# Splitting of value rows and skip products moved off GpSimd in a gated S4 and PEER kernel

## The chip, the cores and the metric

The kernel runs on one NeuronCore of a Trainium2 chip. The core has five engines, each with an instruction stream of its own that it works through in order: TensorE (PE in the profile, its weight loads PEld), VectorE (DVE), ScalarE (ACT), GpSimd (POOL) and SyncE (SP), whose queue issues nearly all DMA transfers here. Streams meet only through semaphores. The metric is the device time of one execution in microseconds, lower being better. Before the change, three runs gave 1459.42, 1458.82 and 1459.39 us, a median of 1459.39 us.

## The reference

One sequence of 2048 tokens with 576 channels, all in fp32, goes through two blocks, and a gate per token mixes what they give:

```python
x = A_u                                             # (1, 2048, 576)
g = sigmoid((x * gate_w).sum(-1, keepdims=True))
a = irfft(rfft(K, 4096) * rfft(u, 4096))[:L] + u * Dskip   # S4: K from A, B, C, dt
# PEER: 32 heads, two sets of 64 subkeys, 64 * 64 = 4096 experts
q = einsum("nd,dhc->nhc", x, w_q)                   # two halves of 128
i1, t1 = top2(q1 @ k1.T);  i2, t2 = top2(q2 @ k2.T)
top_s, top_e = top2(of the four sums t1 + t2, and their experts)
b = einsum(softmax(top_s), gelu(x . u[top_e]), v[top_e])
out = g * a + (1 - g) * b
```

Two places matter here. The *skip product* is `u * Dskip`, one number per channel, added to the convolution. The *value rows* are `v`, 4096 rows of 576 numbers, one row per expert; the sum over the chosen experts weighs them.

## The kernel before, in words

**Products in halves.** TensorE works in fp16. An fp32 operand is scaled and split into a high half (the fp16 rounding) and a low half (the fp16 rounding of what is left); a product is then high x high, high x low and low x high. Tiles named `…hl` hold both halves. The high half is written by ScalarE (`vhl<-vhl,sci`), the low half by VectorE as scaled source minus high half in one instruction (`SCALAR_TENSOR_TENSOR`).

**Stages.** For about 900 us TensorE computes all scores (`s` groups) and the products of every token with every expert's `u` row (`a` groups; evicted as `go`, stored to `g_d` in DRAM), each group on two halves of 64 rows of the array that run beside each other. Between them run the convolution's Fourier stages; the product of the two spectra is made by `products`, whose result waits as `z_d` in DRAM. After `products`, `freq` opens the pool `ab` (L1426) and starts the last stage while the last `a` groups still run.

**The last stage** goes through 16 token tiles of 128 tokens in the order 0, 15, 1, 14 and so on, two tiles making a pair. For each tile, `prep` loads `gl` (two tiles of 1 MB, `gl_0` and `gl_1`), builds one-hot matrices on VectorE for each of four quarters of the heads (`A`, `Be`, and `Bg`, which is `Be` times the weights), has ScalarE apply Gelu to `gl`, and lets TensorE make `S = Bg x A` for the quarter in PSUM, by which VectorE multiplies `gl`. The first two quarters' one-hots are built ahead of the Gelu; those of quarter q+2 come behind the four multiplications of quarter q. Then `gl` is split into `wh_0` (ScalarE) and `wh_1` (VectorE), and 192 matmuls `o<-vhl,wh` of the tile sum over the experts. For each pair, `y_part` loads two tiles `ya` with the rows of `u`, `yz` and `tf`, multiplies `ya` by `db` (the channels' `Dskip`), waits for the inverse transform's `y` matmuls, adds them to `ya` on VectorE (`ya<-y,iuk,ya`), and ScalarE multiplies by the gate. `finish` adds the experts' sum (`ya<-o,om,ya`) and stores.

**Value rows** come in eight chunks of 512. `v_work` loads chunk c raw into the memory in which chunk c+1 will later be split (the last one into a tile `vs`), so chunk c+1 can't be loaded before chunk c is split. A chunk is four pieces of 128 x 576. The piece's high half is ScalarE's. The low half goes one of two ways, chosen at L1604 for each piece: ScalarE scales the raw piece in place (`vhl<-vhl,sci` with an fp32 result, or `vs<-vs,sci`) and GpSimd subtracts the high half; or VectorE does both in one instruction.

**What sets the order.** The program is written out by a planner that runs when it is built: work is a set of generators resumed by a model clock. Each engine has a model of when it will be free (`S.free`, `V.free`, `G.free`, from the cost functions), `ready(...)` waits until a tile is ready by that model, and a choice such as that of L1604 is made by these numbers. So a choice that falls differently also changes in which order later instructions are written. All engine calls go through the wrapper at L136, all matmuls through L216, and DMAs through L207; groups are told apart by their tiles. Waits between engines follow the data, whatever the order.

Of the kernel before, what the change touches and what calls it, by code (L numbers as in the profile page):

```python
# [140 lines left out]
def body(ctx: ExitStack, tc: tile.TileContext, xT, au, par, logdt, dskip, gatew, wq, kT, uT, vv,  # L141
# [5 lines left out]
    clock = [0.0]  # L147
# [15 lines left out]
    def size(x):  # L163
        n = 1
        for d in x.shape[1:]:
            n *= d
        return n
# [30 lines left out]
    S = Engine(nc.scalar, rdy, clock, key, act_cost)  # L198
    V = Engine(nc.vector, rdy, clock, key, dve_cost)
    G = Engine(nc.gpsimd, rdy, clock, key, lambda op, o, a, k: 0.15 + 0.0021 * size(o))  # L200

    def dma(o, i, q=None):
        t = max(clock[0], rdy.get(key(i), 0.0), queue[0])
        queue[0] = t + 0.45
        wire[0] = max(wire[0], t) + (2 if o.dtype in (F16, BF16) else 4) * o.shape[0] * size(o) / 3.4e5
        rdy[key(o)] = max(rdy.get(key(o), 0.0), wire[0] + 2.2)
        (q or DQ).dma_start(o, i)  # L207

    def mm(o, l, r, start, stop, cost=None):
        m = l.shape[0] > 64, 128 if size(l) > 64 else size(l)  # L210
        if m != tiling[0]:
            tiling[0] = m
            clock[0] += 0.13 if m == (True, 128) else 0.1
        clock[0] += (size(r) * (4 if r.dtype == F32 else 1) / 2400 + 0.003) if cost is None else cost
        rdy[key(o)] = clock[0] + 0.4
        return T.matmul(o, l, r, start=start, stop=stop)  # L216
# [73 lines left out]
    def ready(*xs, late=0.0):  # L290
        while True:
            t = max(rdy.get(key(x), 0.0) for x in xs) + late - clock[0]
            if t <= 0:
                return
            yield t
# [32 lines left out]
    def need(tag, n=1):  # L328
        while tag in banksets:
            lst = sorted(vacant)  # L330
            if held[tag] + n <= caps[tag] and len(lst) >= n and lst[n - 1][0] <= clock[0]:
                return
            yield max(0.2, min(0.3, lst[n - 1][0] - clock[0])) if len(lst) >= n else 0.3
        while True:
            lst = sorted(slots[tag])
            if len(lst) >= n and lst[n - 1] <= clock[0]:
                return
            yield max(0.2, lst[n - 1] - clock[0]) if len(lst) >= n else 0.3
# [6 lines left out]
    def free(tag, *outs, of=None):  # L345
        if of is not None:
            held[tag] -= 1
            vacant.append((max([clock[0]] + [rdy.get(key(x), 0.0) for x in outs]), number[of.tensor.name]))
            return
        if owed[tag]:  # L350
            owed[tag] -= 1
            return
        slots[tag].append(max([clock[0]] + [rdy.get(key(x), 0.0) for x in outs]))

    def done(gen):
        for _ in gen:
            return False
        return True
# [7 lines left out]
    def bank(tag, name):  # L366
        held[tag] += 1
        b = min(vacant)
        vacant.remove(b)
        t = ps.tile([128, 512], F32, tag=f"ps{b[1]}", name=name, bufs=1)  # L370
        number[t.tensor.name] = b[1]
        banks.add(t.tensor.name)
        return t
# [7 lines left out]
    def row(x, name, pool):  # L381
        t = pool.tile([128, D], F32, name=name)
        dma(t, bass.AP(tensor=x.tensor, offset=x.offset, ap=[[0, 128], [1, D]]))
        return t
# [7 lines left out]
    def au_load(a, t):  # L392
        for d, o in au_rows(au, t, a):
            dma(o, d)

    def pair_rows(x, n):

        return bass.AP(tensor=x.tensor, offset=x.offset + n * R1 * D, ap=[[D, R1], [32 * R1 * D, 4], [1, D]])
# [66 lines left out]
    def slot(shape, dt, name):  # L465
        take("slot", name)
        return bp.tile([128] + shape, dt, tag="s", name=name, bufs=9)
# [642 lines left out]
    ab = iota_a = iota_b = None  # L1110
# [288 lines left out]
    def freq():  # L1399
# [17 lines left out]
        KS.__exit__(None, None, None)  # L1417
        v_pool(0, 3)
        spawn(v_work())
        fp = FP.__enter__()  # L1420
        quota(sc=4, wb=5)
# [157 lines left out]
    def v_work():  # L1579
        raw = {}  # L1580

        def load(c):
            raw[c] = vt[c + 1].rearrange("p k z d -> p k (z d)").bitcast(F32) if c < 7 else slot([4, D], F32, "vs")
            r = 512 * c
            dma(raw[c], vv[r:r + 512].rearrange("(k p) d -> p k d", p=128))

        for c in range(8):
            while not vnormed or c not in vt or (c < 7 and c + 1 not in vt):
                yield 1
            if c not in raw:  # L1590
                if c == 7:
                    yield from need("slot")
                load(c)
            if c + 2 in vt or (c == 6 and done(need("slot"))):
                load(c + 1)
            h = vt[c]
            yield from ready(raw[c])
            for k in range(0, 4, 2):
                for j in (k, k + 1):
                    S.activation(h[:, j, 0, :], raw[c][:, j, :], AF.Copy, scale=sv[0])  # L1600
                yield from ready(h)
                for j in (k, k + 1):
                    x = raw[c][:, j, :]
                    if G.free < clock[0] + 1 and S.free < V.free:  # L1604
                        S.activation(x, x, AF.Copy, scale=sv[0])
                        yield from ready(raw[c])
                        G.tensor_sub(h[:, j, 1, :], x, h[:, j, 0, :])
                    else:
                        V.scalar_tensor_tensor(h[:, j, 1, :], x, sv[0], h[:, j, 0, :], op0=OP.mult, op1=OP.subtract)
            vhl.append(h)  # L1610
            yield 1
        free("slot", h)
# [80 lines left out]
    def y_part():  # L1693

        def load(p):
            ya = []
            for t in ORDER[2 * p:2 * p + 2]:
                a = oy.tile([128, D], F32, tag="ya", name=f"ya{t}", bufs=4)
                au_load(a, t)
                ya.append(a)  # L1700
            z = oy.tile([128, 4, D], F32, tag="yz", name=f"yz{p}", bufs=1)
            for j in range(4):
                dma(z[:, j], pair_rows(z_d, 4 * p + j))
            tf = oy.tile([128, 4, 64], F32, tag="tf", name=f"tf{p}", bufs=1)
            dma(tf, tf_d[:, 4 * p:4 * p + 4, :])
            return ya, z, tf

        db = row(dskip, "db", oy)
        nxt = load(0)
        for p in range(NT // 2):  # L1710
            ya, z, tf = nxt
            yield from ready(*ya, z, tf, late=4.0)
            for a in ya:
                G.tensor_mul(a, a, db)
            while p and ORDER[2 * p - 2] not in finished:
                yield 0.5
            yield from need("wb", 4)
            pbs = []
            for n in range(2):
                for hh in range(2):  # L1720
                    pb = bank("wb", f"y{p}_{n}_{hh}")
                    for j in range(4):
                        w = 3 - j if n else j
                        mm(pb[32 * j:32 * j + 32, :288], tf[:, w, 32 * n:32 * n + 32], z[:, w, 288 * hh:288 * hh + 288],
                           True, True, 0.13)
                    pbs.append(pb)
            for n, a in enumerate(ya):
                yield from ready(a, *pbs[2 * n:2 * n + 2])
                for hh in range(2):
                    ah = a[:, 288 * hh:288 * hh + 288]  # L1730
                    V.scalar_tensor_tensor(ah, pbs[2 * n + hh][:, :288], iuk, ah, op0=OP.mult, op1=OP.add)
                    free("wb", a, of=pbs[2 * n + hh])
                yield from ready(a)
                t = ORDER[2 * p + n]
                S.activation(a, a, AF.Copy, scale=gA[:, t:t + 1])
                yt[t] = a
            del pbs, pb
            if p + 1 < NT // 2:
                while p and ORDER[2 * p - 1] not in finished:
                    yield 0.5  # L1740
                nxt = load(p + 1)
# [132 lines left out]
    def choose(lst, ok):  # L1874

        near = [g for g in lst[:8] if ok(g)]
        return next((g for g in near if tb_of(g) % 2 != parity[0]), near[0] if near else None)
# [49 lines left out]
    while groups or acts:  # L1927
# [5 lines left out]
        a = choose(acts, a_fit)  # L1933
# [26 lines left out]
    until(lambda: len(placed) == NT)  # L1960
    oy = ctx.enter_context(tc.tile_pool(name="oy", bufs=1))
    spawn(y_part())
    for t in ORDER:
        until(lambda: t in st)
# [71 lines left out]
```

## Time and profile before

| | |
|---|---|
| runs | 1458.82, 1459.39, 1459.42 us; median 1459.39 |
| the profiled execution's own time | 1462.77 us |
| its span in the trace | 1461.0 us |
| TensorE busy | 1427.4 us, 98% of the span |
| VectorE busy | 1196.3 us, 82% |
| ScalarE busy | 837.1 us, 57% |
| GpSimd busy | 520.7 us, 36% |
| mean granted TensorE clock | 0.995 of full speed |

The profiled execution took 1.8 us more than its span and 3.4 us more than the median of the runs. Durations in the trace belong to that one execution. Rows of the trace name the engine, the line, the operation, the tile written and the tiles read (`out<-in`), partitions x elements, and after a count what the engine had waited for just before.

### The profile page before, as it was taken

The numbers are of one execution on the slowest core, as the hardware profiler recorded it, in microseconds if no ns is written. First come the engines' busy times: TensorE is split into PE (matmuls) and PEld (weight loads), VectorE is DVE, ScalarE is ACT, GpSimd is POOL, SyncE is SP. The second block draws the span as 40 slices with busy tenths as digits, with TensorE's granted clock in tenths as the row PEclk, the third lists the DMA queues.
The fourth block names the chain that finished last, engine by engine and source line by source line (L and its number), as shares of the span: only waits on it lengthen the run. The fifth ranks groups of instructions, "written<-read, shape, count | busy, mean of one in ns | idle before, by whom it ended". The sixth has DMA issues, their size and how long they took to land. (4 is left out here: it accounts for less than half of the span.)

```text
span 1461.0 us, 44118 instructions
## 1 busy us (share of the span) xinstructions
PE 1427.4 (98%) x17652; PEld 902.7 (62%) x17654; DVE 1196.3 (82%) x4573; ACT 837.1 (57%) x1452; POOL 520.7 (36%) x513
## 2 busy tenths in 40 slices
PE   7999999999999999999989999999999999999999
PEld 3465566554565665455654444446787887888787
DVE  5888699889889988767789997588989988998860
ACT  6547887987888887754656665574333224223310
POOL 0442265553472663431657899312010010110000
PEclk9999999999999999999999999999999999999999
DMA  9333543333341331248776788577343432442400
GB/s 312 121 113 99 161 129 110 107 119 111 115 147 47 120 109 45 81 141 270 264 252 201 261 269 302 180 242 229 112 148 117 135 119 92 131 148 68 156 9 17
DMA packets 134380, 215.89 MB, mean 148 GB/s; under 512 B 10912, under 2 KB 79904, under 8 KB 127776
## 3 DMA queue, kind: packets, MB, share of 16 engines
q1 hardware_dynamic: 134080, 213.01, 45.1%
q8 instruction: 138, 2.26, 0.6%
q14 instruction: 66, 0.54, 0.1%
q10 hardware_dynamic: 96, 0.07, 0.0%
HBM read 141.74 MB, written 71.30 MB: 146 GB/s over the span
## 5 line engine op out<-in xcount | busy, mean ns | idle before, releaser
L216 PE MATMUL s<-whl,xb 64*128 64x512 f16 x3072 | 469.0, 377 | 0.5 <-ACT k1o L136 0.3
L216 PE MATMUL a<-xb,uhl 64*128 64x512 f16 (+1 forms) x3024 | 457.9, 378 | 0.3 <-DVE go L136 0.2
L216 PE MATMUL o<-vhl,wh 128*128 128x288 f16 x3072 | 388.5, 287 | 0.0
L216 PEld LDWEIGHTS <-wh 128*128 128x128 f16 x3072 | 296.9, 98 | 76.3 <-issue 2.8
L216 PEld LDWEIGHTS <-xb 64*128 64x128 f16 x3456 | 226.5, 94 | 167.5 <-issue 14.5
L216 PEld LDWEIGHTS <-uhl 64*128 64x128 f16 (+1 forms) x3024 | 195.7, 94 | 167.3 <-issue 9.7
L136 ACT ACTIVATE wh<-gl,s_wg 128x1024 f16<-128x1024 f32 x64 | 68.7, 1137 | 195.6 <-DVE gl L136 195.6
L136 POOL TENSOR_TENSOR CS<-CS,ex 128x512 f32<-128x512 f32 x72 | 90.7, 1293 | 167.1 <-DVE ex L136 167.1
L136 POOL TENSOR_TENSOR ya<-ya,db 128x576 f32<-128x576 f32 x16 | 29.7, 1864 | 336.6 <-DMA ya<-in_au_dram 282.8
L216 PE MATMUL s<-wrem,xb 64*128 64x512 f16 x384 | 122.2, 376 | 0.0
L216 PE MATMUL a<-xb,wrem 64*128 64x512 f16 (+1 forms) x380 | 120.8, 379 | 0.0
L136 ACT ACTIVATE go<-a,i_a 128x512 f32<-128x512 f32 x97 | 66.2, 683 | 78.6 <-PE a L216 54.2
L136 DVE FIND_INDEX8 i<-m,s 128x8 uint32<-128x64 f32 x520 | 104.8, 221 | 0.0
L136 DVE SCALAR_TENSOR_TENSOR wh<-gl,s_wg,wh 128x1024 f16<-128x1024 f32 x64 | 91.5, 1459 | 13.4 <-ACT wh L136 13.4
L136 DVE TENSOR_TENSOR gl<-S,gl 128x256 f32<-128x256 f32 x256 | 90.3, 415 | 13.3 <-PE S L216 7.2
L136 POOL TENSOR_TENSOR e<-aN,rt 128x512 f32<-128x512 f32 x72 | 84.0, 1187 | 46.9 <-PE kb L216 46.8
L136 DVE FIND_INDEX8 i<-m,sx 128x8 uint32<-128x64 f32 x504 | 99.3, 217 | 0.0
L136 DVE MAX8 m<-s 128x8 f32<-128x64 f32 x520 | 74.2, 214 | 26.5 <-PE s L216 22.5
L136 DVE TENSOR_TENSOR Bg<-Be,vals 128x1024 f16<-128x1024 f16 x128 | 87.2, 722 | 2.2
L136 ACT ACTIVATE gl<-gl 128x1024 f32<-128x1024 f32 x64 | 63.6, 1045 | 43.6 <-DMA gl<-g_d 43.6
L136 DVE TENSOR_TENSOR A<-iota_a,vals 128x2048 f16<-128x2048 f16 x64 | 78.4, 1224 | 0.0
L136 ACT ACTIVATE CS<-CS 128x1024 f32<-128x1024 f32 x72 | 74.6, 1050 | 6.3 <-DVE CS L136 6.1
(209 smaller groups left out, 2435.0 us busy)
## 6 DMA issues: line engine op xcount, KB each, us to landing
g_d<-go SPq DMA_DIRECT2D x128, 256.0 KB, 2.5
gl<-g_d SPq DMA_DIRECT2D x32, 1024.0 KB, 5.6
wq<-in_wq_dram SPq DMA_DIRECT2D x16, 1152.0 KB, 6.1
su_d<-us SPq DMA_DIRECT2D x32, 288.0 KB, 2.6
sk_d<-k1o SPq DMA_DIRECT2D x32, 288.0 KB, 2.8
ui<-su_d SPq DMA_DIRECT2D x16, 576.0 KB, 4.2
ki<-sk_d SPq DMA_DIRECT2D x16, 576.0 KB, 5.7
vn<-in_vv_dram SPq DMA_DIRECT2D x32, 288.0 KB, 4.3
```

Of the source, the lines that this page charges most:

```text
L136: return f(*a, **k)
L216: return T.matmul(o, l, r, start=start, stop=stop)
```

## The change

Two conditions are edited. In `v_work`, a piece may take the way over ScalarE and GpSimd only as long as `ab` hasn't been opened, which is to say before `products` has ended. Chunks 2 to 7 of the value rows are all split behind it. In `y_part`, the product of `ya` with `db` is issued on VectorE in place of GpSimd.

```diff
@@ v_work
                     x = raw[c][:, j, :]
-                    if G.free < clock[0] + 1 and S.free < V.free:
+                    if ab is None and G.free < clock[0] + 1 and S.free < V.free:
                         S.activation(x, x, AF.Copy, scale=sv[0])
                         yield from ready(raw[c])
                         G.tensor_sub(h[:, j, 1, :], x, h[:, j, 0, :])
                     else:
                         V.scalar_tensor_tensor(h[:, j, 1, :], x, sv[0], h[:, j, 0, :], op0=OP.mult, op1=OP.subtract)
@@ y_part
             for a in ya:
-                G.tensor_mul(a, a, db)
+                V.tensor_mul(a, a, db)
```

Over the whole program this takes from GpSimd 9 subtractions and 16 products, and from ScalarE 9 scalings in place (7 of `vhl`, 2 of `vs`); VectorE gets 9 low halves and 16 products. By the planner's numbers one eviction of an `a` group (`go`) moves from VectorE to ScalarE. TensorE and SyncE have the same instructions as before; SyncE's are in the same order too.

The first place is VectorE's stream from the end of the first token tile to the one-hots and first multiplications of the second; `vhl_16491` is chunk 6 of the value rows (raw in `vhl_16492`), `vhl_16492<-vs` chunk 7. Before:

```order
L136 SCALAR_TENSOR_TENSOR vhl_16491<-vhl_16492,sci,vhl_16491 128x576
L136 TENSOR_TENSOR A_0_17224<-iota_a,vals 128x2048
L136 TENSOR_TENSOR Be_0_17226<-iota_b,vals 128x1024
L136 TENSOR_TENSOR Bg_0_17228<-Be_0_17226,vals 128x1024 x2
L136 TENSOR_TENSOR A_1_17231<-iota_a,vals 128x2048
L136 TENSOR_TENSOR Be_1_17233<-iota_b,vals 128x1024
L136 TENSOR_TENSOR Bg_1_17235<-Be_1_17233,vals 128x1024 x2
L136 SCALAR_TENSOR_TENSOR vhl_16491<-vhl_16492,sci,vhl_16491 128x576
L136 SCALAR_TENSOR_TENSOR vhl_16492<-vs,sci,vhl_16492 128x576
L136 TENSOR_SCALAR go_2_3_17362<-a_2_3_17278,i_a 128x512
L136 SCALAR_TENSOR_TENSOR vhl_16492<-vs,sci,vhl_16492 128x576
L136 TENSOR_TENSOR gl_0_17220<-S_0_0_17383,gl_0_17220 128x32x8
```

After:

```order
L136 SCALAR_TENSOR_TENSOR vhl_16491<-vhl_16492,sci,vhl_16491 128x576 x2
L136 TENSOR_TENSOR A_0_17242<-iota_a,vals 128x2048
L136 TENSOR_TENSOR Be_0_17244<-iota_b,vals 128x1024
L136 TENSOR_TENSOR Bg_0_17246<-Be_0_17244,vals 128x1024 x2
L136 TENSOR_TENSOR A_1_17249<-iota_a,vals 128x2048
L136 TENSOR_TENSOR Be_1_17251<-iota_b,vals 128x1024
L136 TENSOR_TENSOR Bg_1_17253<-Be_1_17251,vals 128x1024 x2
L136 SCALAR_TENSOR_TENSOR vhl_16492<-vs,sci,vhl_16492 128x576 x4
L136 TENSOR_TENSOR gl_0_17238<-S_0_0_17381,gl_0_17238 128x32x8
```

All of chunk 6 now stands ahead of the one-hots, all four pieces of chunk 7 behind them, and the eviction `go_2_3` has left VectorE.

The second place is ScalarE's stream at the same point, up to the Gelu of the second tile (`gl<-gl`). Before:

```order
L136 ACTIVATE vhl_16492<-vhl_16492,sci 128x576
L136 ACTIVATE vhl_16492<-vs,sci 128x576 x2
L136 ACTIVATE go_2_2_17292<-a_2_2_17188,i_a 128x512
L136 ACTIVATE vs<-vs,sci 128x576
L136 ACTIVATE vhl_16492<-vs,sci 128x576 x2
L136 ACTIVATE go_1_1_17330<-a_1_1_17244,i_a 128x512
L136 ACTIVATE vs<-vs,sci 128x576
L136 ACTIVATE gl_0_17220<-gl_0_17220 128x1024 x2
L136 ACTIVATE gl_1_17221<-gl_1_17221 128x1024 x2
```

After:

```order
L136 ACTIVATE vhl_16492<-vs,sci 128x576 x4
L136 ACTIVATE go_2_2_17289<-a_2_2_17182,i_a 128x512
L136 ACTIVATE go_1_1_17322<-a_1_1_17219,i_a 128x512
L136 ACTIVATE go_2_3_17353<-a_2_3_17273,i_a 128x512
L136 ACTIVATE gl_0_17238<-gl_0_17238 128x1024 x2
L136 ACTIVATE gl_1_17239<-gl_1_17239 128x1024 x2
```

The scalings in place are gone from ahead of the Gelu, and `go_2_3` has come in.

The third place is the skip product in the steady part of the last stage, here of the fourth pair on VectorE. Before, the products of all pairs stand on GpSimd one behind the other (here those of the first two pairs, behind chunk 7), and the stream holds nothing else from there to its end:

```order
L136 TENSOR_TENSOR vhl_16492<-vs,vhl_16492 128x576 x2
L136 TENSOR_TENSOR ya_17554<-ya_17554,db 128x576
L136 TENSOR_TENSOR ya_17559<-ya_17559,db 128x576
L136 TENSOR_TENSOR ya_17947<-ya_17947,db 128x576
L136 TENSOR_TENSOR ya_17952<-ya_17952,db 128x576
```

After, on VectorE, between the one-hots of the last quarter and the multiplications by `S_3`:

```order
L136 TENSOR_TENSOR Bg_3_19534<-Be_3_19532,vals 128x1024 x2
L136 TENSOR_TENSOR gl_0_19315<-S_2_0_19567,gl_0_19315 128x32x8
L136 TENSOR_TENSOR gl_1_19316<-S_2_0_19567,gl_1_19316 128x32x8
L136 TENSOR_TENSOR gl_0_19315<-S_2_1_19584,gl_0_19315 128x32x8
L136 TENSOR_TENSOR gl_1_19316<-S_2_1_19584,gl_1_19316 128x32x8
L136 TENSOR_TENSOR ya_19357<-ya_19357,db 128x576
L136 TENSOR_TENSOR ya_19362<-ya_19362,db 128x576
L136 TENSOR_TENSOR gl_0_19315<-S_3_0_19637,gl_0_19315 128x32x8
```

So a pair's two products now stand in line with VectorE's other work, and nothing of the last stage is left on GpSimd. TensorE's stream differs in two stretches: seven row halves of the last `a` groups stand ahead of the second tile's first `S` in place of behind it, and in the first four tiles of the last stage the `o` matmuls are shared out differently between the `S` and `y` groups. From the fifth tile on it is the same.

## The prediction

> **What bounds the kernel now.** I read the page's busy shares first, then windows of the stage that the change touches, then the waits of TensorE in it.
>
> ```profile
> PE 1427.4 (98%) x17652; PEld 902.7 (62%) x17654; DVE 1196.3 (82%) x4573; ACT 837.1 (57%) x1452; POOL 520.7 (36%) x513
> ...
> core 0: us, PE busy (x) PEld busy (x) DVE busy (x) ACT busy (x) POOL busy (x), PEclk, DMA share, GB/s
> 1105.00:1162.00 57.00, 57.00 (x674) 46.20 (x673) 50.71 (x81) 17.88 (x18) 3.74 (x2) 1.00 0.37 119
> 940.00:970.00 30.00, 28.16 (x323) 13.70 (x319) 24.19 (x33) 19.89 (x27) 5.73 (x4) 1.00 0.84 281
> ```
>
> TensorE bounds it. In a pair's period of the last stage (the 1105 row) it is busy 57.00 of 57.00 us, while VectorE has 6.3 us to spare there. Where the value rows are split (the 940 row) TensorE loses 1.84 us in 30. The edited instructions run on other engines, so the change can pay only what TensorE waits for today and can cost only new waits. TensorE's timeline from 943 us to the end shows four waits of over 0.3 us, all for the one-hots `Bg` of VectorE:
>
> ```profile
> 963.74 0.20 PE L216 MATMUL S<-Bg,A 128*128 128x64 f16 x1 [0.36 <-DVE Bg L136]
> 965.41 1.10 PE L216 MATMUL S<-Bg,A 128*128 128x64 f16 x31 [1.48 <-DVE Bg L136]
> ...
> 1001.72 0.59 PE L216 MATMUL a<-xb,wrem 64*128 64x512 f16 x2
> 1003.68 0.20 PE L216 MATMUL S<-Bg,A 128*128 128x64 f16 x1 [1.37 <-DVE Bg L136]
> 1004.28 1.10 PE L216 MATMUL S<-Bg,A 128*128 128x64 f16 x31 [0.40 <-DVE Bg L136]
> 1005.22 5.51 PE L216 MATMUL o<-vhl,wh 128*128 128x288 f16 x30
> ...
> 1031.69 1.10 PE L216 MATMUL S<-Bg,A 128*128 128x64 f16 x31 [0.39 <-DVE Bg L136]
> 1085.06 1.09 PE L216 MATMUL S<-Bg,A 128*128 128x64 f16 x31 [0.41 <-DVE Bg L136]
> 1085.99 3.84 PE L216 MATMUL o<-vhl,wh 128*128 128x288 f16 x30
> ```
>
> The first gap is 0.36 + 1.48 = 1.84 us (the third quarter's `S` of tile one), the second 1.37 + 0.40 = 1.77 us (the same of tile two). Behind the second, 30 `o` matmuls took 5.51 us; the same 30 behind the small wait at 1085 took 3.84. The granted clock says why:
>
> ```profile
> 1005.50:1006.00 0.50, 0.50 (x5) 0.30 (x2) 0.50 (x2) 0.00 (x0) 0.00 (x0) 0.50 0.00 0
> 1008.50:1009.00 0.50, 0.50 (x5) 0.33 (x4) 0.46 (x5) 0.00 (x0) 0.00 (x0) 0.69 0.81 277
> ```
>
> TensorE ran at half clock from about 1005.5 to 1008.7 us, which cost 5.51 - 3.84 = 1.67 us. So all that can be won is 1.84 + 1.77 + 1.67 + 0.39 + 0.41 = 6.1 us, 0.4% of the time.
>
> **What the moved instructions cost, and what they stop costing.**
>
> ```profile
> L136 DVE SCALAR_TENSOR_TENSOR vhl<-vhl,sci,vhl x21: 803/812/1834, 913.0 to 993.4; 128x576 f16<-128x576 f32 x21
> L136 POOL TENSOR_TENSOR ya<-ya,db x16: 1397/1906/2487, 1010.5 to 1362.5; 128x576 f32<-128x576 f32 x16
> L136 DVE TENSOR_TENSOR tt<-tt 128x512 f32<-128x512 f32 x9 | 10.2, 1129 | 0.6
> ...
> 947.23 1.29 DVE L136 TENSOR_TENSOR Bg<-Be,vals 128x1024 f16<-128x1024 f16 x2
> 962.98 2.38 DVE L136 TENSOR_TENSOR Bg<-Be,vals 128x1024 f16<-128x1024 f16 x2
> 963.15 1.66 POOL L136 TENSOR_TENSOR vhl<-vhl,vhl 128x576 f16<-128x576 f32 x1 [8.23 <-ACT vhl L136]
> ...
> 1121.55 2.48 DVE L136 SCALAR_TENSOR_TENSOR wh<-gl,s_wg,wh 128x1024 f16<-128x1024 f32 x2 [0.94 <-ACT wh L136]
> 1133.64 3.63 DVE L136 SCALAR_TENSOR_TENSOR wh<-gl,s_wg,wh 128x1024 f16<-128x1024 f32 x2
> 1133.92 2.27 POOL L136 TENSOR_TENSOR ya<-ya,db 128x576 f32<-128x576 f32 x1 [0.76 <-DVE Bg L136]
> ```
>
> The first rows give minimum, median and maximum ns. A low half is 0.81 us on VectorE, so nine more are 9 x 0.81 = 7.3 us. But a GpSimd product that runs beside VectorE holds it up by about its own length: the pair of `Bg` at 962.98 took 2.38 us beside a GpSimd subtraction, 1.29 without one; the pair of `wh` at 1133.64 took 3.63 beside a skip product, 2.48 without one. That is 1.09 and 1.15 us for each. Taking nine subtractions off GpSimd so gives VectorE back up to 9 x 1.09 = 9.8 us, and one eviction has left VectorE too. Its load in the splitting stage is about what it was (between 7.3 us more, were there no hold-up, and 2.5 less); I take none.
>
> A skip product in fp32 on VectorE isn't in the trace. From below it is the low half of the same size, 0.81 us; from above the fp32 row of 512 columns, 1.13 x 576/512 = 1.27 us, which includes what hold-up those had. I take 0.8, since the low half too reads two operands of this very size: 16 x 0.8 = 13 us over the last stage (20 at the upper end), against 16 x 1.15 = 18 us of hold-up gone. For a pair that is 1.6 to 2.5 us more and 2.3 less, in a period with 6.3 us free. The cost on the path is nothing, covered by VectorE's spare time:
>
> ```profile
> DVE ya L136 <- PE o L216: 16.3, 10, 1.9
> DVE wh L136 <- ACT wh L136: 9.4, 10, 0.9
> DVE gl L136 <- PE S L216: 5.5, 6, 1.2
> ```
>
> These are VectorE's waits over the five periods from 1105 to 1390 us, 31.2 us or 6.2 a period, half of them for TensorE itself. Without this cover each us would come back as a TensorE wait.
>
> The skip products now make VectorE wait in order for the DMA that brings `ya`; queued behind them stand the multiplications by `S_3`, and TensorE waits for `wh` behind these.
>
> ```profile
> 1131.69 1.47 POOL L136 TENSOR_TENSOR ya<-ya,db 128x576 f32<-128x576 f32 x1 [52.16 <-DMA ya<-in_au_dram]
> 1145.96 2.76 DVE L136 TENSOR_TENSOR gl<-S,gl 128x256 f32<-128x256 f32 x8
> ```
>
> GpSimd had its second tile by 1133.92 at the latest; the place on VectorE is inside the run of eight that starts at 1145.96, about 13 us later. No wait there: 0.
>
> **First gap.** ScalarE's and VectorE's rows ahead of it:
>
> ```profile
> 952.79 2.09 ACT L136 ACTIVATE vhl<-vhl,sci 128x576 f32<-128x576 f32 x3
> 956.20 3.90 ACT L136 ACTIVATE gl<-gl 128x1024 f32<-128x1024 f32 x4
> ```
>
> The three scalings in place directly ahead of the Gelu go. The high halves that take their place in line wait for four low halves on VectorE, so I count 1.7 of the 2.09 us as won. Then the `Bg` pair that TensorE waited for loses its hold-up of 1.09 us: 1.7 + 1.09 = 2.8 us, against a gap of 1.84. Closed: 1.84 us, about 1 us in hand.
>
> **Second gap.** Its chain today:
>
> ```profile
> 993.40 0.81 DVE L136 SCALAR_TENSOR_TENSOR vhl<-vhl,sci,vhl 128x576 f16<-128x576 f32 x1
> 994.25 0.78 ACT L136 ACTIVATE vhl<-vs,sci 128x576 f16<-128x576 f32 x1 [4.10 <-DVE vhl L136]
> 996.17 3.88 ACT L136 ACTIVATE gl<-gl 128x1024 f32<-128x1024 f32 x4
> 1000.08 1.08 DVE L136 TENSOR_TENSOR gl<-S,gl 128x256 f32<-128x256 f32 x3 [1.46 <-ACT gl L136]
> 1002.93 1.29 DVE L136 TENSOR_TENSOR Bg<-Be,vals 128x1024 f16<-128x1024 f16 x2
> ...
> gl<-g_d SPq DMA_DIRECT2D x1, 1024.0 KB, 9.1
> ```
>
> Chunk 6's last low half stands behind both one-hots, so ScalarE sits 4.10 us and the Gelu starts at 996.17. It ends at 1000.05; the last `Bg` ends at 1004.22, 4.17 us later. In the new order chunk 6 is done before the one-hots and the scalings are out of line, so ScalarE is held by nothing of the split; what is late next is the second `gl` load (issued at 986.92, landed 996.0) and the eviction `go_2_3` that has come in. With TensorE 1.84 us ahead, the stores ahead of that load, and the load, move up by as much, to 994.2; the Gelu of the first tile can fill the time before. It then ends at 996.6 to 997.1 and the last `Bg` at 1000.8 to 1001.3. TensorE, 1.84 us earlier, comes for it at 1002.31 - 1.84 = 1000.5. A gap of 0.3 to 0.8 stays; I take 0.5 and a gain of 1.77 - 0.5 = 1.3 us.
>
> **Half clock.** A gap of half a us did not bring it: at 1031.69 and 1085.06, 0.4 us, 30 `o` took 3.84 behind the latter. I count its 1.67 us as won. The Trainium skill's TensorE: Matmul & The Clock Gate, Part 1 (The HAM clock gate), speaks against this: the clock falls after an idle window of some 3.4 us and the windows run free of the kernel. No gap here is that long, the 1.84 us of the first was followed by full clock (1.00 in the 940 row), and the 1.77 of the second by half. By that rule the drop hangs on more than the gap's length, and the sum would be without the 1.67 us.
>
> **Small gaps.** The 0.39 and 0.41 us come from VectorE being late by that much. The first pair's skip products leave GpSimd beside it; I take half, 0.4 us.
>
> Sum: 1.84 + 1.3 + 1.67 + 0.4 = 5.2 us. The profiled execution took 1462.77 us, 1.8 over its span and 3.4 over the median; it would become 1457.6, and the median 1459.39 - 5.2 = 1454.2 us. Differences under 0.2% (2.9 us) can hardly be told from none here.
>
> **The rivals.**
>
> *The drop isn't the gap's doing* (the page's rule, as a mechanism of this kernel: it falls on the same stretch or another one). Gains 1.84 + 1.3 + 0.4 = 3.5, so 1455.9. For it: the equal gap at 963 without a drop. Against it: the drop began right with the end of the second gap.
>
> *The second gap stays.* The `gl` load lands no earlier than today's 996.0, its Gelu ends near 998, the last `Bg` at 1002.2, and the gap is again 1.7 us against a TensorE that comes at 1000.5; the half clock then stays as well. Gain 1.84, so 1457.5. For it: the load took 9.1 us in a stretch of heavy DMA traffic (0.84 in the 940 row). Against it: ScalarE's 4.10 us wait is certainly gone.
>
> *VectorE becomes the bound* (slower). In the steady periods a pair costs it 1.6 to 2.5 us more, none is returned, and the skip products stand where TensorE's next `wh` hangs. Were its 6.2 us no real cover, as half of it is waiting for TensorE, seven periods would cost up to 7 x 2.5 = 17 us and at 1 us each 7: with 3.5 gained, 1463 to 1473, say 1465. It decides once `ya` lands over 13 us later or VectorE's slack ahead of `wh` is under 1.6 us. Against it: the returned hold-up, and TensorE's 57.00 of 57.00.
>
> **How the numbers follow.** The forecast 45%, the drop apart 20%, the second gap 23%, the slower case 10%, and 2% for a little more than the sum (all gaps gone, 1453.3). The first, second and last lie under 1456.5: faster 0.64 after a little spread over the bounds. The third gives same, 0.26, with what spreads from the others; slower 0.10. The range goes from 1452.8 (all 6.1 us, and half a us for the runs) to 1459.6 (no change), leaving out the slower case and little else.
>
> **What would show it.** Right: no waits on `Bg` near 962 and under 0.8 us near 1000, granted clock 1.00 from 1000 to 1010, `Bg` pairs at 1.29 throughout, GpSimd idle through the last stage, `ya<-ya,db` on VectorE near 0.8 us without a DMA wait, and 57.00 of 57.00 for TensorE in the steady periods. Wrong: a clock drop elsewhere, ScalarE waiting for `gl<-g_d` ahead of the second Gelu, or new waits of TensorE on `wh` or `y` after 1020. The `y` matmuls too come some 4 us earlier, at 1017, and their table `tf` with them, as far as SyncE's stores have moved up.

## The result and the profile after

The changed kernel takes 1452.66 us (median of six runs, 1451.91 to 1457.09), against 1459.41 us for the kernel before on the same chip: a ratio of 0.9957, 95% interval 0.9944 to 0.9971. That is 6.75 us less, where the prediction had 5.2; the time lies 0.14 us under the low end of its range. On a second chip both were run again: 1453.40 against 1460.59 us, ratio 0.9953 (0.9938 to 0.9968), 7.2 us less.

The page's busy shares of the profiled execution (span 1450.1 us, 1451.91 us in all), and the windows that the prediction showed of before, with one more:

```profile
PE 1422.8 (98%) x17654; PEld 902.6 (62%) x17654; DVE 1193.5 (82%) x4597; ACT 830.3 (57%) x1444; POOL 477.1 (33%) x488
```
```profile
core 0: us, PE busy (x) PEld busy (x) DVE busy (x) ACT busy (x) POOL busy (x), PEclk, DMA share, GB/s
1105.00:1162.00 57.00, 57.00 (x689) 46.30 (x686) 50.79 (x85) 17.88 (x18) 0.00 (x0) 1.00 0.36 119
940.00:970.00 30.00, 30.00 (x365) 15.16 (x363) 26.62 (x45) 17.71 (x24) 0.00 (x0) 1.00 0.86 281
1000.00:1010.00 10.00, 10.00 (x108) 8.20 (x106) 9.90 (x21) 4.27 (x4) 0.00 (x0) 1.00 0.79 211
```

TensorE is busy in all of 940 to 970 us and runs at full clock from 1000 to 1010, where before it was busy for 8.24 of the 10 us at a granted clock of 0.83. VectorE's load in a steady period is what it was, 50.79 us after 50.71 (150.39 after 150.98 over the three windows from 1105 to 1276 us), though a pair has two more instructions there: what it got and what GpSimd no longer takes from it cancel.

TensorE's timeline at the places of the four gaps:

```profile
958.77 1.14 PE L216 MATMUL S<-Bg,A 128*128 128x64 f16 x32
...
995.12 0.59 PE L216 MATMUL a<-xb,wrem 64*128 64x512 f16 x2
995.64 0.20 PE L216 MATMUL S<-Bg,A 128*128 128x64 f16 x1
996.11 1.10 PE L216 MATMUL S<-Bg,A 128*128 128x64 f16 x31 [0.27 <-DVE Bg L136]
...
1024.58 1.10 PE L216 MATMUL S<-Bg,A 128*128 128x64 f16 x31 [0.21 <-DVE Bg L136]
...
1076.37 1.13 PE L216 MATMUL S<-Bg,A 128*128 128x64 f16 x32
1077.34 3.84 PE L216 MATMUL o<-vhl,wh 128*128 128x288 f16 x30
```

The first gap is gone. Of the second 0.27 us are left, of the third 0.21, of the fourth nothing.

**The two profiles can't be subtracted as they stand.** Their spans differ by 10.9 us, more than the medians do. In the profile of before TensorE had also waited 1.72 us for `vo` at 913 us and run at half clock behind it, ahead of anything that the change moves; its first `S` starts at 955.12, that of after at 950.58. Executions of one kernel differ by a few us in that way before the last stage begins. So below, an execution is measured from the start of the first `S` to the end of the span, and cut at two places on TensorE's timeline: the first `o` and the first `y`; the last cut is the last `S`. From that to the end it was 57.7 us in every kernel. (The `before again` row is from an experiment below.)

| us | first S to first o | to first y | to last S | first S to end of span |
|---|---|---|---|---|
| before | 50.10 | 16.69 | 381.39 | 505.88 |
| before again | 50.46 | 16.28 | 381.89 | 506.33 |
| after | 46.47 | 15.02 | 380.37 | 499.52 |
| after again | 46.47 | 15.02 | 380.00 | 499.20 |

By this the change is worth 6.4 to 7.1 us, as the medians have it: 3.6 to 4.0 in the first part (the two gaps), 1.3 to 1.7 in the second (the half clock), 1.0 to 1.9 in the third. In `before again` the half clock begins at 999.99 us, ahead of the first `o` at 1000.83, so some 0.4 us of it stand in its first part.

### The profile page after: what moved, and what is told of

The parts are those of the page before. It is cut to its first block, busy times and chain, and to the rows that moved or that the text cites. A ratio compares the mean times of both kernels' runs of the same rounds, so it can differ in the third digit from the quotient of the medians.

```text
span 1450.1 us, 44027 instructions
## 1 busy us (share of the span) xinstructions
PE 1422.8 (98%) x17654; PEld 902.6 (62%) x17654; DVE 1193.5 (82%) x4597; ACT 830.3 (57%) x1444; POOL 477.1 (33%) x488
## 4 chain that ended last, share of the span: by engine, by line
PE 86%; DMA 5%; DVE 4%; issue 1%; SPq 1%; ACT 1%; POOL 1%; ACTq 0%; POOLq 0%; DVEq 0%
PE a L216 25%; PE o L216 24%; PE s L216 21%; PE S L216 4%; PE kb L216 2%; PE pr L216 2%; PE wb L216 2%; DMA wq<-in_wq_dram 1%; SPq L207 1%; PE kP L216 1%; PE y L216 1%; DVE i L136 1%; PE pv L216 1%; DVE m L136 1%; PE u L216 1%
## 5 line engine op out<-in xcount | busy, mean ns | idle before, releaser
L136 DVE SCALAR_TENSOR_TENSOR wh<-gl,s_wg,wh 128x1024 f16<-128x1024 f32 x64 | 79.7, 1278 | 10.4 <-ACT wh L136 10.4
L136 DVE TENSOR_TENSOR Bg<-Be,vals 128x1024 f16<-128x1024 f16 x128 | 82.7, 688 | 2.2
L216 PEld LDWEIGHTS <-A 128*128 128x128 f16 x2048 | 70.1, 97 | 6.4 <-issue 2.8
```

Of the source, the lines that this page charges most:

```text
L136: return f(*a, **k)
```

## Experiments

Each kernel was timed in five rounds beside the kernel before on the same chip (before: 1461.48 us for the first four, 1460.59 for the next four, 1461.82 for the last four), and profiled once.

**The split edit alone.** The diff against the kernel before:

```diff
-                    if G.free < clock[0] + 1 and S.free < V.free:
+                    if ab is None and G.free < clock[0] + 1 and S.free < V.free:
```

> Only the edit of v_work; the skip products stay on GpSimd. Theory (the gain is that of the two gaps on Bg and of the half-clock stretch behind the second, all in the stage where the value rows are split): 5 to 6 us less than before, the waits at 963 and 1002 us gone or under 0.5 us, full clock from 1000 to 1010; the small waits of 0.4 us at 1031 and 1085 stay. Rival (the gain comes from GpSimd being free beside VectorE through the last stage): under 2 us less than before.

1457.89 us, ratio 0.9982 (0.9968 to 0.9995): 3.6 us less. The parts of the last stage are 46.46, 15.03 and 384.36 us, 503.50 in all. The first two parts are those of the changed kernel: both gaps shut, no half clock. But of the 5.3 us that they give, 2.7 are lost in the third (384.36 against 381.39 and 381.89). TensorE's timeline of this kernel behind the first `y`:

```profile
1016.49 2.15 PE L216 MATMUL y<-yz,tf 128*32 128x288 f32 x32
1018.57 1.14 PE L216 MATMUL S<-Bg,A 128*128 128x64 f16 x32
1019.54 0.90 PE L216 MATMUL o<-vhl,wh 128*128 128x288 f16 x6
1021.62 1.12 PE L216 MATMUL S<-Bg,A 128*128 128x64 f16 x32 [1.17 <-DVE ya L136]
1022.58 4.57 PE L216 MATMUL o<-vhl,wh 128*128 128x288 f16 x36
1028.66 0.20 PE L216 MATMUL S<-Bg,A 128*128 128x64 f16 x1 [1.50 <-DVE Bg L136]
1029.26 1.10 PE L216 MATMUL S<-Bg,A 128*128 128x64 f16 x31 [0.40 <-DVE Bg L136]
```

TensorE, 5.3 us ahead of before at `y` (61.5 us behind the first `S` in place of 66.8), now waits there for VectorE: 1.17 us until `ya<-y` frees a bank and 1.90 for the third tile's `Bg`. Half of the gain is lost again one tile on. Theory right on the gaps, wrong in taking them for the edit's whole effect.

**The skip edit alone.**

```diff
-                G.tensor_mul(a, a, db)
+                V.tensor_mul(a, a, db)
```

> Only the edit of y_part; the value rows are split as before. Theory: 0.4 to 0.8 us less than before, which the runs can hardly tell from nothing: both gaps on Bg of 1.8 us and the half clock behind the second stay; VectorE's pairs of wh take 2.48 us throughout. Rival: 4 us less or more. Where VectorE has no room for the products: 3 us more or worse.

1458.72 us, ratio 0.9986 (0.9975 to 0.9996): 2.8 us less by the medians. In the profile 50.10, 15.02 and 379.99 us. The third part has lost all its waits, 1.4 to 1.9 us. Both gaps stay, and the second this time has no half clock behind it:

```profile
1000.84 0.20 PE L216 MATMUL S<-Bg,A 128*128 128x64 f16 x1 [1.36 <-DVE Bg L136]
1001.44 1.10 PE L216 MATMUL S<-Bg,A 128*128 128x64 f16 x31 [0.40 <-DVE Bg L136]
1002.38 3.84 PE L216 MATMUL o<-vhl,wh 128*128 128x288 f16 x30
```

So by the profile the skip edit is worth about 1.5 us by itself; the rest of its median lies within the scatter. That a gap of 1.76 us at this place passes without half clock was not expected.

**The kernel before, again** (unchanged).

> The kernel before, unchanged, for a second profile. In the first one TensorE also waited 1.72 us for vo at 913 us, ahead of anything that the change moves, and ran at half clock for some 7 us behind it; the changed kernel's profile has neither. Theory: that was this one execution (it took 3.4 us more than the median), so it is absent here, and the time is near 1459.4 with a mean clock of 0.998 or so. Rival: it is in every execution of the kernel before, and the changed kernel gained there too. The gaps at 963 and 1002 us are in both, by both.

1461.13 us, ratio 0.9998 (0.9987 to 1.0010). The wait for `vo` is 0.56 us here, without half clock behind it, so the first profile's was of its execution. The two gaps are as they were, and half clock stands behind the second again. But the mean clock over the runs is 0.995, not 0.998: this profile has half clock near 597, 686 and 744 us too, ahead of the change and in other executions elsewhere. All fourteen profiles have one such stretch or more between 590 and 760 us, at places that change, and they go with the scatter: over the 35 runs of before beside these four kernels, the runs with a lower mean clock are the longer ones (correlation -0.74).

**The gap put back.** In the changed kernel, for `t == ORDER[1]` and `q == 2` (the two runs at the end of this section have `range(1)`, and `ORDER[0]` with `range(5)`, in place of these):

```diff
         V.tensor_tensor(out=Be, in0=iota_b[:, None].to_broadcast([128, 8, 64, 2]), in1=ib(1, 64), op=OP.is_equal)
+        if t == ORDER[1] and q == 2:
+            for _ in range(3):
+                nc.vector.tensor_tensor(out=Be, in0=iota_b[:, None].to_broadcast([128, 8, 64, 2]), in1=ib(1, 64), op=OP.is_equal)
```

> The changed kernel, with VectorE building Be three times more, to the same result, ahead of the Bg that the third S of the second tile waits for: 3 x 0.6 = 1.8 us. TensorE's wait there grows from about 0.4 to 2.1 us, the length that it had before or a little more. Theory (a gap of 1.8 us at this place brings the half clock): about 1.8 us for the gap and 1.7 for the clock, 3.5 in all over the changed kernel, and a granted clock under 0.9 in the 3 us behind it. Rival (the drop before came from elsewhere): 1.8 us more and full clock.

1457.76 us, ratio 0.9983 (0.9971 to 0.9995): 4.4 us over the changed kernel's 1453.40 on that chip, or 3.5 when each is taken against its own series of the kernel before. TensorE's timeline, and windows behind the gap (the granted clock is the third number from the end):

```profile
998.78 0.24 PE L216 MATMUL S<-Bg,A 128*128 128x64 f16 x1 [1.98 <-DVE Bg L136]
999.38 1.81 PE L216 MATMUL S<-Bg,A 128*128 128x64 f16 x31 [0.36 <-DVE Bg L136]
```
```profile
1000.00:1002.50 2.50, 2.50 (x30) 1.97 (x28) 2.46 (x5) 0.00 (x0) 0.00 (x0) 0.50 0.61 122
1002.50:1005.00 2.50, 2.50 (x12) 1.59 (x11) 2.46 (x8) 0.00 (x0) 0.00 (x0) 0.50 0.73 223
```

A gap of 2.34 us brought half clock, and for 6.8 us, not 3.4. From first `S` to end of span the kernel takes 504.02 us, 4.5 to 4.8 over the changed one. That is the theory's case, if anything over its 3.5: a gap of this length here costs more than itself.

**The changed kernel, again** (unchanged).

> The changed kernel, unchanged, on the same chip as the next ones. Theory: as on the first chip, 6 to 7 us less than before (some 1454 to 1455 where before takes 1461), with no wait on Bg over 0.5 us in the profile and no half clock between 995 and 1010 us. Rival (part of the first result was the chip's or the executions' scatter): 4 to 5 us less.

1453.40 us, 7.2 us less than before; no gap over 0.3 us and no half clock behind the first `S`. The first result holds on a second chip.

**The order of the changed kernel, the skip products on GpSimd.**

```diff
+                V.eng = nc.gpsimd
                 V.tensor_mul(a, a, db)
+                V.eng = nc.vector
```

The planner still counts them as VectorE's, so every engine's order is that of the changed kernel; only the products themselves are on GpSimd.

> The order of the changed kernel on every engine, with the skip products issued on GpSimd at the same places. It tells the engine from the order. Theory (the order, in which 18 o matmuls stand between y and the next S, is what keeps TensorE fed here, the engine is worth about 1 us): 1 to 1.5 us slower than the changed kernel, by a wait on Bg of 1 to 1.5 us near 1025 us. Rival (the engine is what counts): as slow as the split edit alone, 3 us over the changed kernel, with a wait for ya behind y.

1454.00 us, ratio 0.9957 (0.9940 to 0.9975): 0.6 us over the changed kernel, not told from it, and less than the 1 to 1.5 expected. The parts are 46.47, 15.68 and 380.67 us; the wait for `Bg` near 1026 us is 0.40 us, not 1 to 1.5, and the second part holds a wait of 0.58 us at `y`.

**The order of the split edit alone, the skip products on VectorE.** The same exchange of the engine, on the kernel with only the split edit:

```diff
+                G.eng = nc.vector
                 G.tensor_mul(a, a, db)
+                G.eng = nc.gpsimd
```

> The order of the kernel with the split edit alone on every engine, with the skip products issued on VectorE at the places where they were issued on GpSimd: the other corner of the same square. Theory: S right behind the first y still waits for the bank that ya<-y sets free, now behind the two products, but VectorE comes there 2.3 us earlier without GpSimd's hold-up: waits of 0.3 us for ya and some 0.7 for Bg in place of 1.17 and 1.90, so about 2 us less than the split edit alone. Rival: no gain over the split edit alone.

1456.77 us, ratio 0.9970 (0.9957 to 0.9984): 1.1 us less than the split edit alone by the medians, 0.2 against each one's own series of the kernel before: not told from it, where 2 less was expected. The parts are 46.46, 15.81 and 384.33 us. The wait for `ya` is gone, but that for `Bg`, expected at 0.7, has grown from 1.90 to 2.58 us, with half clock from 1028.11 us on:

```profile
1027.83 0.20 PE L216 MATMUL S<-Bg,A 128*128 128x64 f16 x1 [2.18 <-DVE Bg L136]
1028.43 1.81 PE L216 MATMUL S<-Bg,A 128*128 128x64 f16 x31 [0.40 <-DVE Bg L136]
```

With these two runs, order and engine can be told apart. The third part, first `y` to last `S`:

| us | skip products on GpSimd | on VectorE |
|---|---|---|
| order of the split edit alone | 384.36 | 384.33 |
| order of the changed kernel | 380.67 | 380.37, 380.00 |

The 384.33 holds up to 1.7 us of half clock (half of the 3.41 us from 1028.11 to 1031.52). So the order is worth 3.7 us with GpSimd's products and 2.3 to 4.3 with VectorE's, the engine 0.3 to 0.7 us in the changed order and not over 1.7 in the other. What the skip edit does for the split edit it does mostly through the order. (At the fourth gap, near 1085 us, either is enough: it is gone in both of these runs.) The order differs where TensorE goes on behind the first `y`, here in the kernel with the skip edit alone, which has the changed kernel's order at this place:

```profile
1017.40 2.15 PE L216 MATMUL y<-yz,tf 128*32 128x288 f32 x32
1019.48 2.38 PE L216 MATMUL o<-vhl,wh 128*128 128x288 f16 x18
1021.69 1.13 PE L216 MATMUL S<-Bg,A 128*128 128x64 f16 x32
```

Eighteen `o` matmuls, 2.2 us of work, stand between `y` and the next `S`, and 42 in place of 36 ahead of the third tile's third `S`. What they cover is not VectorE's work alone. ScalarE and VectorE at the third tile, first in the kernel with the split edit's order and the products on VectorE, then in the changed kernel:

```profile
1022.19 2.00 ACT L136 ACTIVATE gl<-gl 128x1024 f32<-128x1024 f32 x2 [1.64 <-DMA gl<-g_d]
1024.23 1.09 DVE L136 TENSOR_TENSOR gl<-S,gl 128x256 f32<-128x256 f32 x3 [3.22 <-ACT gl L136]
...
1018.34 2.00 ACT L136 ACTIVATE gl<-gl 128x1024 f32<-128x1024 f32 x2 [1.90 <-DMA gl<-g_d]
```

The `Bg` that TensorE waits for stands behind VectorE's multiplications by `S_0`, these wait for the Gelu, and the Gelu for the tile's second `gl` load. From this Gelu's start (1022.19 and 1018.34 us) to the second row of the `S` that needs `Bg` (1028.43 and 1024.58) it is 6.24 us in both. The split edit alone brings `y` nearer to the first `S` by 5.3 us, but this Gelu by only 2.3 (it starts 66.8 us behind the first `S` in place of 69.1, at 1021.81 in place of 1024.25), so it now starts 5.3 us behind `y` and not 2.3 as before. In the split edit's order with the products on VectorE, TensorE asks for `Bg` 9.3 us behind the start of `y`; in the changed order 12.1 us. That the rows shown, and no other difference of the order, carry the whole of it was not tried by itself.

**Does VectorE's spare time cover more work?** The changed kernel with one `A` more, to the same result:

```diff
         V.tensor_tensor(out=A, in0=iota_a[:, None].to_broadcast([128, 8, 128, 2]), in1=ib(0, 128), op=OP.is_equal)
+        if t in ORDER[4:] and q in (2, 3):
+            nc.vector.tensor_tensor(out=A, in0=iota_a[:, None].to_broadcast([128, 8, 128, 2]), in1=ib(0, 128), op=OP.is_equal)
```

> The changed kernel, with VectorE building A once more, to the same result, in the third and fourth quarter of tiles five to sixteen: 4 x 1.14 = 4.6 us more on VectorE in each pair's period, where it had 6.2 us of waits before. Theory (the spare time of VectorE is real cover): not over 1 us more than the changed kernel. Rival (half of the spare time is waiting for TensorE and no cover): 1.5 us a pair and more, over 9 us in all.

1461.42 us, ratio 1.0009 (0.9998 to 1.0019): 8.0 us over the changed kernel. The theory falls. The third part is 387.88 us, 7.9 over the 380 of the kernels without a wait there, which is 1.3 us for each of six pairs out of the 4.6 put in. The steady period in windows and VectorE's waits from 1105 to 1390 us:

```profile
1105.00:1162.00 57.00, 56.12 (x662) 44.94 (x660) 54.10 (x87) 17.89 (x18) 0.00 (x0) 1.00 0.36 119
```
```profile
DVE wh L136 <- ACT wh L136: 9.5, 10, 0.9
DVE ya L136 <- PE o L216: 4.1, 5, 0.9
DVE gl L136 <- issue: 3.0, 4, 0.8
```

VectorE still waits 16.6 us over the five periods while TensorE already waits for it in every tile. Spare time in sum isn't spare time at a place: the 9.5 us for `wh` lie where nothing else can be pulled ahead in an engine that works in order.

**Chunks 2 to 5 by the old way, 6 and 7 by the new.**

```diff
-                    if ab is None and G.free < clock[0] + 1 and S.free < V.free:
+                    if (ab is None or c < 6) and G.free < clock[0] + 1 and S.free < V.free:
```

> The changed kernel, with the way over ScalarE and GpSimd left open for chunks 2 to 5 (five pieces take it, all before or during the first token tile) and closed for 6 and 7. Theory (the split edit pays by two gaps that are shut one by one, and the first brought no half clock): the first gap is back with 1.84 us, the second shut; 1.8 us slower than the changed kernel, full clock from 940 to 1010. Rival (the gaps hang together, TensorE being early at the second what it won at the first): the second closes anyhow when the first stays, and what is lost is under 1 us, or both are back.

1457.29 us, ratio 0.9967 (0.9954 to 0.9980). The parts are 48.53, 15.77 and 381.00 us. The first gap is back as it was, 0.36 and 1.48 us, the second is down to 0.26, and the granted clock is full behind both. That is the theory. From first `S` to the end the kernel loses 3.5 to 3.8 us against the changed one, though, not 1.8: further waits of 0.32 (`Bg`, the quarter behind the second gap), 0.20 (`tf` at `y`) and 0.67 us (`Bg` near 1028) have come in.

**Chunks 6 and 7 by the old way, 2 to 5 by the new** (`c >= 6` in place of `c < 6`).

> The other half: the way over ScalarE and GpSimd left open for chunks 6 and 7 (four pieces take it), closed for 2 to 5. Theory: the first gap is shut, the second back with 1.8 us or more, since TensorE now comes 1.84 us earlier to the same late Bg (up to 3.6), and with it the half clock in many executions (1.7 us): 3 to 5 us slower than the changed kernel. Rival (the half clock came from both gaps together): 1.8 us slower and full clock.

1456.88 us, ratio 0.9968 (0.9955 to 0.9981). The parts are 48.57, 15.80 and 380.00 us. The first gap is shut; the second is back with half clock:

```profile
998.51 0.20 PE L216 MATMUL S<-Bg,A 128*128 128x64 f16 x1 [1.22 <-DVE Bg L136]
999.11 1.12 PE L216 MATMUL S<-Bg,A 128*128 128x64 f16 x18 [0.40 <-DVE Bg L136]
```
```profile
997.50:1000.00 2.50, 1.09 (x19) 1.00 (x20) 2.46 (x7) 0.52 (x1) 0.00 (x0) 0.78 0.36 105
1000.00:1002.50 2.50, 2.50 (x27) 1.85 (x25) 2.46 (x5) 0.00 (x0) 0.00 (x0) 0.53 0.24 79
```

It is 1.62 us, no longer than before although TensorE comes earlier: VectorE and ScalarE, relieved in the first tile, come earlier too. Each gap belongs to the chunks beside it. From first `S` to the end the kernel loses 2.6 to 2.9 us against the changed one, a little less than the 3 to 5 expected.

**A short gap at the second tile** (one `Be` more).

> As the run with three more Be ahead of the second tile's third S, now with one: 0.6 us. Theory (a short gap there costs its own length and brings no half clock): 0.6 us or less over the changed kernel, with a mean clock of 0.998 as it has. Rival (any gap at this place brings it): 2.3 us, mean clock 0.996.

1455.92 us, ratio 0.9959 (0.9946 to 0.9973); in the profile a gap of 0.93 us at the place, full clock behind it, 500.40 us from first `S` to end, 0.9 to 1.2 over the changed kernel. The mean clock over its nine runs was 0.996, but in the profile all that it lost is near 600 and 746 us, ahead of the place. The short gap costs its length.

**A gap at the first tile** (five `Be` more, at `ORDER[0]`).

> The changed kernel with five more Be ahead of the first tile's third S, where TensorE came 0.9 us after the last Bg: 3.0 - 0.9 = 2.1 us of gap, about as long as that of the run with three more at the second tile, which was followed by half clock, and 0.3 us longer than the kernel before had here, which was not. Theory (half clock hangs on the gap's length): 2.1 us for the gap and 1.7 or more for the clock, the granted clock near 0.5 somewhere between 957 and 965 us, mean clock 0.996 or less. Rival (what counts is where the gap falls): 2.1 us and full clock.

1457.88 us, ratio 0.9977 (0.9967 to 0.9987). TensorE's timeline and the windows behind it:

```profile
962.39 0.20 PE L216 MATMUL S<-Bg,A 128*128 128x64 f16 x1 [2.59 <-DVE Bg L136]
962.99 1.81 PE L216 MATMUL S<-Bg,A 128*128 128x64 f16 x31 [0.40 <-DVE Bg L136]
```
```profile
962.50:965.00 2.50, 2.10 (x34) 1.78 (x34) 2.50 (x6) 0.00 (x0) 0.00 (x0) 0.54 0.11 30
965.00:967.50 2.50, 2.50 (x20) 1.05 (x18) 2.46 (x5) 0.00 (x0) 0.00 (x0) 0.77 0.00 0
```

The gap came out at 2.99 us, and half clock followed at the place where 1.84 us never brought it (the two profiles of the kernel before, that of the skip edit alone, and that with chunks 2 to 5 by the old way). From first `S` to the end it is 503.75 us, 4.2 to 4.6 over the changed kernel. Length counts, not the place alone; the last section says in what way.

## Why the prediction came out as it did

*What bounds the kernel* was right: TensorE, with all that could be won in its waits and its clock behind 943 us. The bound of 6.1 us, though, held only the idle time of the waits above 0.3 us in one profile; the measured gain is 6.4 to 7.1.

*First gap, 1.84 us*: right, by its own mechanism. The two steps ahead of it, from the timelines of ScalarE and VectorE in the changed kernel:

```profile
949.53 3.90 ACT L136 ACTIVATE gl<-gl 128x1024 f32<-128x1024 f32 x4
...
956.59 1.29 DVE L136 TENSOR_TENSOR Bg<-Be,vals 128x1024 f16<-128x1024 f16 x2
```

The Gelu of the first tile starts 2.1 us earlier against the first `S` (1.08 us behind it before, at 956.20 after 955.12; 1.05 ahead of it now, at 949.53 before 950.58), and the `Bg` pair takes 1.29 us in place of 2.38. It ends 0.9 us ahead of TensorE; the prediction said about 1.

*Second gap, 1.3 us*: right in kind; 1.5 to 1.8 were won, since a residue of 0.27 us at most was left where 0.5 was taken.

*Half clock, 1.67 us*: the 16.69 and 16.28 us of the second part became 15.02, so 1.3 to 1.7 us, and the reason held in both profiles of the changed kernel. But the term was taken as certain, and it is partly luck of the execution: of four profiles with a gap of 1.62 to 1.77 us at this place three have the half clock (both of before and that with chunks 6 and 7 by the old way), that of the skip edit alone has none. The rival *the drop isn't the gap's doing* lost as to this place, but it was right that more than the gap's length decides; see the last section.

*Small gaps, 0.4 us*: this is the mis-sized term. The third part gave 1.0 to 1.9 us. The skip edit alone takes them all away, 379.99 against 381.39 and 381.89. The prediction had looked only at the idle time in the two rows of about 0.4 us and halved it. Such a wait costs more than its row says, since it cuts the `S` group in two: from 1031.10 us, where this `S` starts, to the next `o` at 1032.63 it is 1.53 us, against 0.97 for an `S` in one piece (1029.19 to 1030.16 in the changed kernel). And the other profile of before has waits of 0.35 and 0.39 us at the first of these places, not one.

*The skip products at no cost, about 0.8 us each*: right in size and sign, with a reason that was too strong. The group of the changed kernel:

```profile
L136 DVE TENSOR_TENSOR ya<-ya,db x16: 746/748/754, 1014.3 to 1363.4; 128x576 f32<-128x576 f32 x16
```

They take 0.75 us, and none waited for its DMA. But VectorE's waits are no general cover; the run with 4.6 us more shows that, though it put its work at other places. VectorE's unchanged busy time speaks for the hold-up given back as the cover. Two readings there were off: GpSimd's work doesn't hold VectorE up by its own length (1.09 us beside one of 1.66, 1.15 beside one of 2.27), and of VectorE's 31.2 us of waits 21.8, over two thirds and not half, were for TensorE.

*Left out altogether*: the order of TensorE's own stream. The prediction carried the split edit's gains straight to the end, as if what TensorE won at the second tile could not be lost at the third. With the split edit alone 2.7 us of 5.3 are lost there again. What TensorE meets there is the third tile's `gl` load, which came earlier by less than TensorE did. That the sum held all the same is owed to the order that the skip edit makes, with 18 `o` matmuls behind `y`, a difference that got no term; as to the mechanism that is luck.

The rival *the second gap stays* didn't come: the load of `gl` moved up, and landed 37.0 us behind the first `S` in place of 40.9. *VectorE becomes the bound* didn't either, but it was nearer than its 10%: 4.6 us more a period, ahead of `Bg`, make the kernel as slow as before.

## What to carry to other kernels

Before adding up gains along a bound engine's stream, follow each to the next place where that engine meets the others: work won at one wait arrives early at the next, and whether it is kept there is decided by what that place really waits for, here a load, and by what stands in between, here independent matmuls. In a kernel whose order is planned from modelled engine times, moving an instruction to another engine may matter through the order that it makes and hardly through the engine; run the new order with the old engine to tell. And compare stretches between marks that both traces have, not spans, when the executions scatter as much as the change moves.

## What was not expected of the hardware

A gap in TensorE's work well below the half-clock stretch's own length can bring it. Taking a gap as the sum of the waits in a row at one place, from 890 us on in all fourteen profiles: of the gaps up to 0.93 us none was followed by half clock, of thirteen from 1.17 to 1.90 us six were, and all three from 2.34 to 2.99 us were. A stretch lasts 3.41 us, or twice that, and costs up to half its length.

What counts beside the length is where the gap falls. In one profile the starts of the stretches are whole multiples of 3.413 us apart: in that of before they are 684.54, 913.24 and 1005.39 us, 67.00 and 27.00 such steps; the same holds in every profile with more than one. TensorE's busy time and the granted clock there, in windows cut by this step, around the first and the second gap:

```profile
core 0: us, PE busy (x) PEld busy (x) DVE busy (x) ACT busy (x) POOL busy (x), PEclk, DMA share, GB/s
961.03:964.44 3.41, 2.54 (x23) 0.99 (x20) 3.38 (x5) 3.07 (x6) 1.29 (x1) 1.00 0.85 308
964.44:967.85 3.41, 2.44 (x45) 1.67 (x46) 3.41 (x7) 0.99 (x2) 0.37 (x1) 1.00 0.31 89
967.85:971.26 3.41, 3.41 (x56) 1.91 (x52) 3.38 (x7) 1.36 (x2) 0.36 (x1) 1.00 0.04 13
1001.98:1005.39 3.41, 1.65 (x36) 1.20 (x35) 3.38 (x8) 0.69 (x1) 0.00 (x0) 1.00 0.41 119
1005.39:1008.80 3.41, 3.41 (x16) 2.18 (x15) 3.35 (x7) 0.00 (x0) 0.00 (x0) 0.50 0.47 157
```

The first gap falls into two windows, with 0.87 and 0.97 us of idle time, and the clock stays full; the second falls into one, with 1.76 us, and the next window runs at half clock. The skip edit alone had 0.41 and 1.35 us in two windows at the second gap. From 890 to 1440 us in all profiles, each of the six full-clock windows with 1.72 us of idle time or more was followed by half clock, of four with 1.42 to 1.60 two were, and of those with less one alone (0.87 us, at 912 us with the split edit's order and the products on VectorE). The Trainium skill's TensorE: Matmul & The Clock Gate, Part 1 (The HAM clock gate), gives a window of some 3.4 us that runs free of the kernel, and with that these profiles agree; that the clock falls after a whole idle window does not agree, since about half of one was enough here. Why 0.87 us was enough once stays open.

A GpSimd subtraction and a product, each of two operands of 128 x 576, held up the pair of VectorE instructions beside it by 1.09 and 1.15 us in the two places that the prediction shows; the skip product took GpSimd 1.4 to 2.5 us and takes VectorE 0.75. Moving sixteen of them to VectorE left its busy time in a period unchanged, 50.71 and 50.79 us.
